# An adaLN transformer block on one core: MLP slices in groups of two, four, four, two, two, GpSimd's products of Mish regrouped, the last dense slot beside a maximum

## The chip, the core and the metric

The kernel runs on one core of a Trainium2 chip. The metric is the device time of one execution in microseconds (us); less is better. A core has the engines TensorE (PE, with its weight loads PEld), VectorE (DVE), ScalarE (ACT), GpSimd (POOL) and SyncE (SP), each with its own queue of instructions that it takes in order; SP's queue here holds the loads and stores. The matrix products go into PSUM, of which there are eight banks of 128 x 512 fp32.

## The reference

One block with adaptive layer norm: attention over 2048 positions with 32 heads of 16, then an MLP with Mish. Three of the six rows of `mod` shift, scale and gate each half.

```python
mod = (silu(c) @ w_mod)                      # sa, ca, ga, sb, cb, gb
h = layernorm(x) * (1 + ca) + sa             # x: 2048 x 512
q, k, v = (h @ wqkv) split in 32 heads of 16
o = softmax(q @ k.T * 16**-0.5) @ v
x = x + ga * (o @ wo)
h = layernorm(x) * (1 + cb) + sb
u = h @ w1 + b1                              # w1: 512 x 1792
x = x + gb * ((u * tanh(softplus(u))) @ w2)  # w2: 1792 x 512
```

## The kernel before

**Precision.** Dense products are made from a high and a low part of each operand, three matmuls for one. The splitting is a copy (`hi_copy`, L95) and a subtract (`lo_sub`, L98), mostly on GpSimd.

**The main loop.** After a first stage that makes q, k and v there are 32 iterations `n` (4 query blocks of 512 rows by 8 groups of 4 heads) of 16 steps each, T = 512 steps. A step `t` issues four score products (`score`, L507, each followed on ACT by an exp into `pr`, L513), four products for the row maxima of the iteration 20 steps ahead (`max_tile`, L470, each followed on DVE by a reduce, L472), and the products of the probabilities of step t − 2 with the values (`pv`, L531, 8 matmul instructions). `neg_max` (L481) joins the maxima of an iteration, a transposition (L487) turns them. Scores and maxima take turns in a ring of six PSUM banks; the banks "ms" and "acc" hold the dense unit at work and the values' sums.

**Dense work beside it.** A score or maximum uses 64 of PE's 128 rows. On the other 64 runs a half-height dense matmul (`mm_half`, L132), six "slots" in most steps, written between the scores and maxima. The order within the step is `mine` with `beside` in `step`: maximum, dense, score, dense and so on. A dense unit (128 or 512 columns by three partial products) of 12 slots fills four steps, a smaller one two. The first dense matmul of the next half is made to wait for `cur["after"]`, the instruction that reads the product in the last slot's place.

**The MLP as units.** The MLP of query blocks 0 to 2 runs in the main loop of the following query block: four `wo` units with their transpositions (`tr_unit`, L840), then 14 `up` units, one for each slice `f` of 128 columns of w1, and `down` units, one for each group of slices and each of four row blocks. An end of a unit calls `fin`: a bias on ACT for an up (L726), a copy on ACT (L882) and an add on GpSimd (L883) for a down. The MLP of the last query block, and the last downs of block 2 (`held`), run in the tail, whole-height (`mm`, L126).

**Mish.** With e = exp(min(u, 10)), Mish is u times e(e+2) / (e(e+2)+2). The stages of an up that ends at half step h stand in hooks, `at(h + i, stage)`, two half steps to a step: clamp (GpSimd, L732) at +1, power (ACT, L738) +3, product (GpSimd, L746 to L748) +4, log (ACT, L751) +9, inverse (ACT, L754) +13, quotient (GpSimd, L763 to L767) +13, then the places and the split of the result (L95, L98) +16 and +18. Within a half step the hooks run in the order in which they were entered. The order of each engine's instructions is that of the program text; no scheduler moves them.

**Around it.** `evac` copies an iteration's output `ot`, spreads its row sums over DMA (`rb`) and multiplies, copies and subtracts in `norm` (L574, L95, L98) on GpSimd. Weights come split from DRAM by `load_wo`, `load_w1`, `load_w2`, entered at the ends of certain units.

Of the kernel before, what the change touches and what calls it, by code (L numbers as in the profile page):

```python
# [18 lines left out]
def adaln_block(ctx: ExitStack, tc: tile.TileContext, x, wqkv, wo, w1, b1, w2, c, w_mod, out):  # L19
# [442 lines left out]
    def max_tile(n, j, s, qs, kb):  # L462

        if n not in mxs:
            mxs[n] = ap.tile([P, 2, 8, 4], F32, tag="mx", name="mx", bufs=2)

        def product():
            kt, qt = ka[(2 * n + j) % NR], qa[(2 * n + j) % NR]
            pm = ring()
            nc.tensor.matmul(pm, qt[64 * s:64 * s + 64, qs * P:(qs + 1) * P], kt[64 * s:64 * s + 64, kb * TB:(kb + 1) * TB],  # L470
                             start=True, stop=True)
            nc.vector.tensor_reduce(out=mxs[n][:, s, 4 * j + qs, kb:kb + 1], in_=pm, op=ALU.max, axis=AX.X)  # L472

        return product

    def neg_max(n):

        mx = mxs.pop(n)
        mm = ap.tile([P, 4, 2, 4], F32, tag="mm", name="mm", bufs=2)
        for v in range(2):  # L480
            nc.vector.tensor_reduce(out=mm[:, :, v, :], in_=mx.rearrange("p s (j q) k -> p (s j) q k", j=2), op=ALU.max,  # L481
                                    axis=AX.X)
        ats.setdefault(16 * n + 16 - PRO, []).append(lambda: max_rows(n, mm))
# [19 lines left out]
    def score(n, j, s, kc):  # L503
        def product():
            kt, qt = ka[(2 * n + j) % NR], qa[(2 * n + j) % NR]
            p_ = ring()
            nc.tensor.matmul(p_, kt[64 * s:64 * s + 64, kc * P:(kc + 1) * P], qt[64 * s:64 * s + 64, :],  # L507
                             start=True, stop=True)
# [4 lines left out]
            e = nc.scalar.activation(pr, p_, AF.Exp, scale=SCALE)  # L513
            if (h, b) in exps:
                tc.declare_no_dep(e.ins, exps[h, b].ins, reason="the values' product between them reads it")
            exps[h, b] = e
            pts[16 * n + kc, 2 * j + s] = pr
            return e
        return product
# [19 lines left out]
    def evac(n):  # L539
# [30 lines left out]
        if g % 2 == 1 or n == NIT - 2:  # L570
            r = slice(0, P if g % 2 else 64)

            def norm():
                nc.gpsimd.tensor_mul(od[r], od[r], rb[r])  # L574
                oh, ol = o_hl[qb]
                hi_copy("p", oh[r, g // 2, :], od[r])
                lo_sub("p", ol[r, g // 2, :], od[r], oh[r, g // 2, :])
            at(2 * t1 + (29 if g == 1 else 17 if hurry else 23), norm)
# [133 lines left out]
    def mish(f, acc, tail):  # L712
# [15 lines left out]
        def clamp():  # L728
            if tail:
                nc.scalar.activation(buf("ee", 2), b["hb"], AF.Relu, bias=hcap, scale=-1.0)  # L730
            else:
                nc.gpsimd.tensor_scalar(buf("ee", 2), b["hb"], HCAP, 0.0, op0=ALU.min, op1=ALU.add)  # L732
# [7 lines left out]
        def product():  # L740
            hb, ee, rr = b["hb"], b["ee"], buf("rr", 2)
            if tail:
                nc.vector.scalar_tensor_tensor(ee, ee, 2.0, ee, op0=ALU.add, op1=ALU.mult)
                nc.vector.tensor_mul(hb, hb, ee)
            else:
                nc.gpsimd.tensor_scalar(rr, ee, 1.0, 2.0, op0=ALU.mult, op1=ALU.add)  # L746
                nc.gpsimd.tensor_mul(ee, ee, rr)  # L747
                nc.gpsimd.tensor_mul(hb, hb, ee)  # L748
# [7 lines left out]
        def quotient():  # L756
# [5 lines left out]
            else:  # L762
                nc.gpsimd.tensor_scalar(ee, ee, 1.0, 2.0, op0=ALU.mult, op1=ALU.add)  # L763
                nc.gpsimd.tensor_mul(ee, ee, rr)  # L764
                nc.gpsimd.tensor_scalar(ee, ee, -1.0, 2.0, op0=ALU.mult, op1=ALU.add)
                nc.gpsimd.tensor_mul(rr, rr, ee)
# [17 lines left out]
    GROUPS = [list(range(a, min(a + 4, FT))) for a in range(0, FT, 4)]  # L784
    blocks = []

    def block(qb, t0):
# [39 lines left out]
        def tr_unit(i):  # L827
# [7 lines left out]
            def fin(h):  # L835

                def scaled():
                    hf = mst["p"].tile([P, TB], F32, tag="ee", name="hf2", bufs=2).rearrange("p (k m) -> p k m", m=P)
                    for k in range(DK):
                        nc.scalar.activation(hf[:, k], acc[:, k * P:(k + 1) * P], AF.Identity,  # L840
                                             scale=modc[:, 3, k:k + 1], bias=modc[:, 2, k:k + 1])
                    s = slice(i * P, (i + 1) * P)
                    hi_copy("p", hx[0][:, :, s], hf)
                    lo_sub("p", hx[1][:, :, s], hf, hx[0][:, :, s])

                at(h, scaled)
# [4 lines left out]
        def up_unit(f, tag):  # L851
# [16 lines left out]
        def down_unit(gi, i, tag=None, acc=None):  # L868
# [8 lines left out]
            if gi == 2 and i == 3 and not held and then:  # L877
                load(cur["h"] + 5, then["wo"], load_wo, range(2))

            def fin(h):  # L880
# [3 lines left out]
                if gi == len(GROUPS) - 1:  # L884
# [5 lines left out]
                    put() if held else at(h + 4, put)  # L890
                if held:
                    return
                if gi < 2 and i == 3:
                    load(h + 1, w2s, load_w2, range(6 + 4 * gi, 10 + 4 * gi))
                if then and gi == 2 and i == 0:
                    load(h + 1, then["y"], lambda j: load_y(qb + 1, j), range(3))
                if then and gi == 2 and i == 3:
                    load(h + 1, then["wo"], load_wo, range(2, DK))
                if then and gi == 3 and i == 0:
                    load(h + 10, then["y"], lambda j: load_y(qb + 1, j), range(3, 4))  # L900
                if then and gi == 3 and i == 3:
# [15 lines left out]
        if qb == NB - 2:  # L917
            mst["held"] = lambda j, acc: down_unit(2 + j // 4, j % 4, None, acc)
# [3 lines left out]
    def all_blocks():  # L922
# [3 lines left out]
        for qb, b in enumerate(blocks):  # L926
            wo, up, down = (b["units"][k] for k in ("wo", "up", "down"))
            before = blocks[qb - 1]["units"]["down"] if qb else lambda gi, i: None
            before(3, 0)
            for i in range(4):  # L930
                wo(i)
            for i in range(1, 4):
                before(3, i)
# [29 lines left out]
    def tail():  # L963
# [42 lines left out]
        for js in ((0, 1), (2,)):  # L1006
# [3 lines left out]
        fins = held((3,))  # L1010
# [102 lines left out]
    def step(t):  # L1113
# [27 lines left out]
        if t >= T:  # L1141
# [6 lines left out]
            return  # L1148
        if tm < T:
# [3 lines left out]
            mine = [x for p in zip(mo, own) for x in p] + own[len(mo):]  # L1153
        else:
# [9 lines left out]
        def emit(product):  # L1164
            e = product()
            if e is not None and cur.pop("want", None):
                cur["after"] = e

        for i in range(max(len(mine), len(beside))):
            if i == len(mine) // 2:  # L1170
                run_hooks(2 * t + 1)
            if i < f:
                last = i + 1 == f
                if i < len(mine) and mine[i] and not last:
                    emit(mine[i])
                for m in beside[i]:
                    mm_half(m, second, cur["first"], bool(second and last and m is beside[i][-1] and not cur["left"]),
                            cur.pop("after", None))
                    cur["first"] = False
                if last:  # L1180
                    cur["want"] = True
                    if i < len(mine):
                        emit(mine[i])
# [149 lines left out]
```

## Time and profile before

| what | value |
|---|---|
| runs | 1756.39, 1763.5, 1764.14 us, median 1763.5 |
| profiled execution, its own time | 1760.91 us |
| its span, first to last instruction | 1759.1 us |
| mean granted TensorE clock | 0.988 |
| DMA, mean over the span | 136 GB/s |
| DVE's reduces of maxima, L472 | 2048 of 682 ns |
| ACT's exps of scores, L513 | 2048 of 606 ns |

The page gives for each engine its busy time and its share of the span. The chain of waits follows the last instruction back to what released it, and gives the share of the span that each engine has on it. A row of a group reads "line engine operation out<-in, shape, xcount | busy us, mean ns of one | idle us of the engine just before them and what ended it". A row of the waits reads "who <- for whom: us in all, times, the longest". A row of the timeline reads "start us, us, engine, line, operation, xcount, [idle before <- releaser]". A row of the windows reads "from:to length", then for each engine its busy time and (xcount), at last the granted clock, the DMA share and GB/s; with a line given, it counts that line's instructions alone.

### The profile page before, as it was taken

What the parts mean: (1) busy time and instruction counts of PE and PEld (TensorE: products, weight loads), DVE (VectorE), ACT (ScalarE), POOL (GpSimd) and SP (SyncE); (2) the same over time, 40 slices, a digit from 0 to 9 for tenths busy, and PEclk for the clock granted to TensorE, in tenths of its full rate; (3) what the DMA queues carried; (4) which work ended last, traced back from release to release, by engine and by line L of the source; (5) the groups of instructions that cost most, each with busy time, mean ns of one, the idle gap of its engine ahead of it and who ended that gap; (6) DMA issues with size and microseconds to landing.
All of it is one profiled execution on the core that took longest, in us unless ns stands there. A gap on an engine that the chain in (4) does not pass through costs nothing.

```text
span 1759.1 us, 32844 instructions
## 1 busy us (share of the span) xinstructions
PE 1703.3 (97%) x12236; PEld 973.7 (55%) x12236; DVE 1423.9 (81%) x2384; ACT 1345.7 (77%) x2593; POOL 921.1 (52%) x898
## 2 busy tenths in 40 slices
PE   6999999999999989999999989999999989999999
PEld 5755655555345555555545555555545555554677
DVE  6988888888888878888878878888878878882367
ACT  6257777777779878888879878888878878888464
POOL 5245234666213497656524597656423696666452
PEclk9999999999999999999999999999999999999999
DMA  7777458777844332434532633524442533423252
GB/s 248 190 232 207 117 162 240 220 224 222 254 105 113 98 90 65 119 98 100 132 106 67 185 101 74 129 82 119 120 99 79 166 91 90 133 63 136 95 215 73
DMA packets 113992, 240.03 MB, mean 136 GB/s; under 512 B 24048, under 2 KB 49648, under 8 KB 107784
## 3 DMA queue, kind: packets, MB, share of 16 engines
q1 hardware_dynamic: 113832, 237.92, 47.6%
q8 instruction: 97, 1.59, 0.4%
q14 instruction: 63, 0.52, 0.1%
HBM read 179.95 MB, written 51.44 MB: 132 GB/s over the span
## 4 chain that ended last, share of the span: by engine, by line
PE 77%; DMA 10%; POOL 4%; ACT 3%; DVE 3%; SPq 2%; issue 1%; POOLq 0%; ACTq 0%; DVEq 0%
PE bk L531 25%; PE ring L470 18%; PE ring L507 17%; PE bk L132 11%; PE ring L126 2%; DMA qscr<-ql 2%; ACT pr L513 2%; PE ring L1047 1%; DVE mx L472 1%; DMA w2scr<-hl 1%; DMA kscr<-ql 1%; PE bk L126 1%; DMA vg<-vscr 1%; DMA hl<-in_B_w 1%; DMA ka<-kscr 1%
## 5 line engine op out<-in xcount | busy, mean ns | idle before, releaser
L472 DVE TENSOR_REDUCE mx<-ring 128x1 f32<-128x512 f32 x2048 | 1273.2, 682 | 225.7 <-PE ring L470 180.6
L513 ACT ACTIVATE pr<-ring 128x512 f32<-128x512 f32 x2048 | 1100.9, 606 | 263.4 <-PE bk L132 148.1
L470 PE MATMUL ring<-ka,qa 64*128 64x512 f32 x2048 | 843.1, 425 | 0.7 <-ACT hf L840 0.4
L507 PE MATMUL ring<-qa,ka 64*128 64x512 f32 x2048 | 725.9, 401 | 7.2 <-ACT pr L513 6.7
L470 PEld LDWEIGHTS ring<-ka,qa 64*128 64x128 f32 x2048 | 369.3, 185 | 408.0 <-DVE mx L472 349.3
L531 PE MATMUL bk<-pr,vg 128*32 128x512 f32 x4096 | 551.8, 611 | 0.0
L507 PEld LDWEIGHTS ring<-qa,ka 64*128 64x128 f32 x2048 | 374.2, 186 | 84.1 <-ACT pr L513 45.8
L132 PE MATMUL bk<-h,w 64*128 64x512 f32 x1008 | 283.0, 413 | 15.2 <-ACT pr L513 15.2
L132 PE MATMUL bk<-w,a_h 64*128 64x512 f32 x576 | 193.8, 416 | 0.8 <-ACT pr L513 0.5
L132 PEld LDWEIGHTS bk<-h,w 64*128 64x128 f32 x1008 | 176.1, 187 | 25.8 <-ACT pr L513 20.8
L531 PEld LDWEIGHTS bk<-pr,vg 128*32 128x32 f32 x4096 | 81.5, 108 | 140.4 <-issue 132.9
L132 PE MATMUL bk<-w,a_l 64*128 64x512 f32 x288 | 113.2, 393 | 0.0
L764 POOL TENSOR_TENSOR ee<-ee,rr 128x512 f32<-128x512 f32 x42 | 53.8, 1280 | 108.5 <-ACT rr L754 107.2
L883 POOL TENSOR_TENSOR y<-yd,y 128x512 f32<-128x512 f32 x40 | 51.8, 1295 | 110.6 <-ACT yd L882 99.4
L732 POOL TENSOR_SCALAR ee<-hb 128x512 f32<-128x512 f32 x42 | 80.7, 1921 | 48.2 <-ACT hb L726 45.2
L132 PEld LDWEIGHTS bk<-w,a_h 64*128 64x128 f32 x576 | 95.5, 184 | 7.1 <-ACT pr L513 3.3
L132 PE MATMUL bk<-w,o_hl 64*128 64x512 f32 x288 | 85.1, 426 | 7.4 <-POOL o_hl L95 6.5
L98 POOL TENSOR_TENSOR a_l<-hb,a_h 128x512 fp32r<-128x512 f32 x53 | 71.7, 1354 | 4.4
L132 PEld LDWEIGHTS bk<-w,o_hl 64*128 64x128 f32 x288 | 51.6, 193 | 12.6 <-POOL o_hl L95 7.8
L574 POOL TENSOR_TENSOR od<-od,rb 128x512 f32<-128x512 f32 (+1 forms) x16 | 20.6, 1289 | 71.3 <-DMA vg<-vscr 57.9
L132 PE MATMUL bk<-h_h,wl 64*128 64x512 f32 x168 | 56.9, 419 | 0.0
L747 POOL TENSOR_TENSOR ee<-ee,rr 128x512 f32<-128x512 f32 x42 | 54.1, 1289 | 3.5
(205 smaller groups left out, 1841.8 us busy)
## 6 DMA issues: line engine op xcount, KB each, us to landing
ka<-kscr SPq DMA_DIRECT2D x124, 384.0 KB
w<-w2scr SPq DMA_DIRECT2D x56, 512.0 KB
w<-w1scr SPq DMA_DIRECT2D x46, 512.0 KB
vg<-vscr SPq DMA_DIRECT2D x32, 552.0 KB
qa<-qscr SPq DMA_DIRECT2D x124, 100.0 KB
kscr<-qh SPq DMA_DIRECT2D x16, 512.0 KB
qscr<-qh SPq DMA_DIRECT2D x32, 256.0 KB
hl<-in_B_w SPq DMA_DIRECT2D x28, 256.0 KB
```

Source lines behind the costliest of these rows:

```text
L98: (nc.gpsimd if eng == "p" else nc.vector).tensor_sub(lo, src, hi.bitcast(F32))
L126: nc.tensor.matmul(acc, l, r, start=start, stop=stop)
L132: i = nc.tensor.matmul(acc, l[64 * g:64 * g + 64], r[64 * g:64 * g + 64], start=start, stop=stop)
L470: nc.tensor.matmul(pm, qt[64 * s:64 * s + 64, qs * P:(qs + 1) * P], kt[64 * s:64 * s + 64, kb * TB:(kb + 1) * TB], start=True, stop=True)
L472: nc.vector.tensor_reduce(out=mxs[n][:, s, 4 * j + qs, kb:kb + 1], in_=pm, op=ALU.max, axis=AX.X)
L507: nc.tensor.matmul(p_, kt[64 * s:64 * s + 64, kc * P:(kc + 1) * P], qt[64 * s:64 * s + 64, :], start=True, stop=True)
L513: e = nc.scalar.activation(pr, p_, AF.Exp, scale=SCALE)
L531: nc.tensor.matmul(accs[n][32 * h:32 * h + 32, :], vgs[n][:, o:o + 32], pts.pop((t, h)), start=(kc == 0), stop=(kc == 15))
L732: nc.gpsimd.tensor_scalar(buf("ee", 2), b["hb"], HCAP, 0.0, op0=ALU.min, op1=ALU.add)
L747: nc.gpsimd.tensor_mul(ee, ee, rr)
L764: nc.gpsimd.tensor_mul(ee, ee, rr)
L883: nc.gpsimd.tensor_add(y[i], yd, y[i])
```

## The change

The text changes in seven places.

1. `GROUPS`: the 14 slices go into groups 0–1, 2–5, 6–9, 10–11, 12–13 instead of 0–3, 4–7, 8–11, 12–13. There are five downs for each row block instead of four; a down of two slices takes two steps, one of four slices four. `all_blocks` queues five ups first, then downs and ups in a new pattern. The tail takes ten held downs instead of eight. Loads of w2, wo and y are entered at other units' ends.
2. Mish on GpSimd: `clamp` is a single min instead of min and add 0; `product` no longer multiplies u by e(e+2); `quotient` is made of a multiply, one tensor_scalar 2 − 2r, a subtract and the two products with u.
3. From up 5 on, power and product stand at +5 and +6 instead of +3 and +4.
4. `step`: where the last dense slot stood beside a score, the score moves one slot ahead and a maximum stands there. `cur["after"]` is then the reduce of that maximum.
5. At the end of a dense unit, the exp of the score in the slot before is held back until `fin` has written the bias or the copy.
6. `neg_max` joins the maxima with one reduce instead of two; `norm`'s three operations go into three hooks; `tr_unit` scales at once.
7. The store of an output row block goes to a hook that `clear` moves past an iteration's end.

**PE.** The first step with dense work beside it (h_h and h_l are the normed input; wh and wl the parts of a weight), before:

```order
L132 MATMUL bk<-h_h,wl 128x512
L470 MATMUL ring<-ka_633,qa_108 128x512
L132 MATMUL bk<-h_l,wh 128x512
L507 MATMUL ring<-qa_106,ka_104 128x512
L132 MATMUL bk<-h_l,wh 128x512
L470 MATMUL ring<-ka_633,qa_108 128x512
L132 MATMUL bk<-h_l,wh 128x512 x2
L507 MATMUL ring<-qa_107,ka_105 128x512
L531 MATMUL bk<-pr_0_1175,vg 32x512
```

and now:

```order
L132 MATMUL bk<-h_h,wl 128x512
L470 MATMUL ring<-ka_633,qa_108 128x512
L132 MATMUL bk<-h_l,wh 128x512
L506 MATMUL ring<-qa_106,ka_104 128x512
L132 MATMUL bk<-h_l,wh 128x512
L506 MATMUL ring<-qa_107,ka_105 128x512
L132 MATMUL bk<-h_l,wh 128x512 x2
L470 MATMUL ring<-ka_633,qa_108 128x512
L534 MATMUL bk<-pr_0_1174,vg 32x512
```

The last score and the last maximum of the dense part have changed places; the count is the same.

**ACT.** Around the end of an up in block 0 (`pr` are the exps of scores), before:

```order
L513 ACTIVATE pr_0_1175<-ring 128x512
L513 ACTIVATE pr_0_1182<-ring 128x512
L513 ACTIVATE pr_1_1176<-ring 128x512
L726 ACTIVATE hb<-bk,b1c 128x512
L513 ACTIVATE pr_1_1183<-ring 128x512
L513 ACTIVATE pr_2_1151<-ring 128x512
L751 ACTIVATE rr<-ee,two 128x512
```

and now, for the first cycle with a down of two slices between two ups, from the bias of up 5 over the inverse of up 4 to the power of up 5:

```order
L514 ACTIVATE pr_2_1183<-ring 128x512
L728 ACTIVATE hb<-bk,b1c 128x512
L514 ACTIVATE pr_0_1174<-ring 128x512
L514 ACTIVATE pr_0_1181<-ring 128x512
L514 ACTIVATE pr_0_1148<-ring 128x512
L755 ACTIVATE rr<-rr 128x512
...
L878 COPY yd<-bk 128x512
L514 ACTIVATE pr_2_1176<-ring 128x512
L514 ACTIVATE pr_2_1183<-ring 128x512
L514 ACTIVATE pr_2_1150<-ring 128x512
L740 ACTIVATE ee<-ee 128x512
```

The bias stands ahead of the last two exps of its step instead of the last one. Eight exps and a copy stand between the inverse and the power.

**GpSimd.** The same cycle before, with quotient, clamp, split and product:

```order
L766 TENSOR_TENSOR rr<-rr,ee 128x512
L767 TENSOR_TENSOR hb<-hb,rr 128x512
L732 TENSOR_SCALAR ee<-hb 128x512
L95 TENSOR_SCALAR a_h<-hb 128x512
L98 TENSOR_TENSOR a_l<-hb,a_h 128x512
L746 TENSOR_SCALAR rr<-ee 128x512
L747 TENSOR_TENSOR ee<-ee,rr 128x512
L748 TENSOR_TENSOR hb<-hb,ee 128x512
L763 TENSOR_SCALAR ee<-ee 128x512
```

and now:

```order
L764 TENSOR_TENSOR ee<-ee,rr 128x512
L765 TENSOR_SCALAR rr<-rr 128x512
L766 TENSOR_TENSOR rr<-rr,ee 128x512
L767 TENSOR_TENSOR hb<-hb,ee 128x512
L768 TENSOR_TENSOR hb<-hb,rr 128x512
L734 TENSOR_SCALAR ee<-hb 128x512
L879 TENSOR_TENSOR y_5257<-yd,y_5257 128x512
L95 TENSOR_SCALAR a_h<-hb 128x512
L98 TENSOR_TENSOR a_l<-hb,a_h 128x512
L748 TENSOR_SCALAR rr<-ee 128x512
L749 TENSOR_TENSOR ee<-ee,rr 128x512
```

The product is one multiply shorter; the quotient ends with the two products, and the clamp of the next up stands right behind it.

The diff, its core:

```diff
@@ max_tile, neg_max @@
-            nc.vector.tensor_reduce(out=mxs[n][:, s, 4 * j + qs, kb:kb + 1], in_=pm, op=ALU.max, axis=AX.X)
+            return nc.vector.tensor_reduce(out=mxs[n][:, s, 4 * j + qs, kb:kb + 1], in_=pm, op=ALU.max, axis=AX.X)
-        for v in range(2):
-            nc.vector.tensor_reduce(out=mm[:, :, v, :], ...)
+        twice = bass.AP(tensor=mx.tensor, offset=mx.offset, ap=[list(mx.ap)[0], [16, 4], [0, 2], [4, 4], [1, 4]])
+        nc.vector.tensor_reduce(out=mm, in_=twice, op=ALU.max, axis=AX.X)
@@ score @@
-        def product():
+        def product(hold=False):
...
-            e = nc.scalar.activation(pr, p_, AF.Exp, scale=SCALE)
+            def power():
+                e = nc.scalar.activation(pr, p_, AF.Exp, scale=SCALE)
...
+            return power if hold else power()
@@ norm (in evac) @@
+            k, d = 2 * t1 + (29 if g == 1 else 17 if hurry else 23), 0 if hurry else 2
+            at(k, lambda: nc.gpsimd.tensor_mul(od[r], od[r], rb[r]))
+            at(k + d, lambda: hi_copy("p", oh[r, g // 2, :], od[r]))
+            at(k + 2 * d, lambda: lo_sub("p", ol[r, g // 2, :], od[r], oh[r, g // 2, :]))
@@ mish @@
-                nc.gpsimd.tensor_scalar(buf("ee", 2), b["hb"], HCAP, 0.0, op0=ALU.min, op1=ALU.add)
+                nc.gpsimd.tensor_scalar_min(buf("ee", 2), b["hb"], HCAP)
...
                 nc.gpsimd.tensor_scalar(rr, ee, 1.0, 2.0, op0=ALU.mult, op1=ALU.add)
                 nc.gpsimd.tensor_mul(ee, ee, rr)
-                nc.gpsimd.tensor_mul(hb, hb, ee)
...
-                nc.gpsimd.tensor_scalar(ee, ee, 1.0, 2.0, op0=ALU.mult, op1=ALU.add)
                 nc.gpsimd.tensor_mul(ee, ee, rr)
-                nc.gpsimd.tensor_scalar(ee, ee, -1.0, 2.0, op0=ALU.mult, op1=ALU.add)
-                nc.gpsimd.tensor_mul(rr, rr, ee)
+                nc.gpsimd.tensor_scalar(rr, rr, -2.0, 2.0, op0=ALU.mult, op1=ALU.add)
+                nc.gpsimd.tensor_sub(rr, rr, ee)
+                nc.gpsimd.tensor_mul(hb, hb, ee)
                 nc.gpsimd.tensor_mul(hb, hb, rr)
@@ up_unit, down_unit @@
-    GROUPS = [list(range(a, min(a + 4, FT))) for a in range(0, FT, 4)]
+    GROUPS = [list(range(a, b)) for a, b in ((0, 2), (2, 6), (6, 10), (10, 12), (12, FT))]
-                for i, s in zip((1, 3, 4, 9, 13, 13, 16, 18), stages):
+                for i, s in zip((1, 3, 4, 9, 13, 13, 16, 18) if f < 5 else (1, 5, 6, 9, 13, 13, 16, 18), stages):
-                    put() if held else at(h + 4, put)
+                    put() if held else at(clear(h + 8), put)
+                more = {(0, 3): (6, 8), (1, 3): (8, 12), (2, 3): (12, 14)}.get((gi, i))
+                if more and held:
+                    w2s.update((k, load_w2(k)) for k in range(*more))
+                elif more:
+                    load(h + 1, w2s, load_w2, range(*more))
@@ all_blocks @@
-            for f in range(6):
+            for f in range(5):
                 up(f)
-            for j in range(8):
-                down(j // 4, j % 4)
-                up(6 + j)
-            for i in range(4 if qb < NB - 2 else 0):
-                down(2, i)
+            for i in range(4):
+                down(0, i)
+                up(5 + i)
+            down(1, 0)
+            up(9)
+            down(1, 1)
+            up(10)
+            down(1, 2)
+            down(1, 3)
+            up(11)
+            down(2, 0)
+            up(12)
+            down(2, 1)
+            up(13)
+            if qb < NB - 2:
+                down(2, 2)
+                down(2, 3)
+                for i in range(4):
+                    down(3, i)
@@ tail @@
-        for js in ((0, 1), (2,)):
+        for js in ((0, 1), (2, 3)):
...
-        fins = held((3,))
+        fins = held((4, 5))
...
-        fins += held((4, 5))
+        fins += held((6, 7))
...
-        for f in held((6, 7)):
+        for f in held((8, 9)):
@@ step @@
+            kinds = [k for p in zip("m" * len(mo), "s" * len(mo)) for k in p] + ["s"] * (len(own) - len(mo))
+            swap = 2 <= f <= len(mine) and kinds[f - 1] == "s" and kinds[f - 2] == "m"
+            if swap:
+                mine[f - 2:f] = mine[f - 1], mine[f - 2]
...
+        ends = second and f and not cur["left"]
...
+                    if swap and ends and i + 2 == f:
+                        held = mine[i](True)
+                    else:
+                        emit(mine[i])
...
-                    cur["want"] = True
-                    if i < len(mine):
-                        emit(mine[i])
-                    if second and not cur["left"]:
+                    if ends:
                         cur["fin"](2 * t + 2)
                         cur["fin"] = None
+                    if held:
+                        held()
+                    cur["want"] = True
+                    if i < len(mine) and mine[i]:
+                        emit(mine[i])
```

More of the change, by code (lines that the diff above doesn't have):

```diff
@@ L512, in product @@
             pr = prs[h][b]
[L513 to L518, printed above, removed]
+            def power():
+                e = nc.scalar.activation(pr, p_, AF.Exp, scale=SCALE)
+                if (h, b) in exps:
+                    tc.declare_no_dep(e.ins, exps[h, b].ins, reason="the values' product between them reads it")
+                exps[h, b] = e
+                pts[16 * n + kc, 2 * j + s] = pr
+                return e
+            return power if hold else power()
         return product
@@ L1148, in step @@
             return
+        swap, held = False, None
         if tm < T:
@@ L1174, in step @@
                 if i < len(mine) and mine[i] and not last:
-                    emit(mine[i])
+                    if swap and ends and i + 2 == f:
+                        held = mine[i](True)
+                    else:
+                        emit(mine[i])
                 for m in beside[i]:
-                    mm_half(m, second, cur["first"], bool(second and last and m is beside[i][-1] and not cur["left"]),
+                    mm_half(m, second, cur["first"], bool(ends and last and m is beside[i][-1]),
                             cur.pop("after", None))
```

52 lines of the change are left out of this document (19 added, 33 removed).

## The prediction, made before the change was run

> **What bounds the kernel now.** I read the busy times and the chain of waits first, for the engine that sets the end.
>
> ```profile
> PE 1703.3 (97%) x12236; PEld 973.7 (55%) x12236; DVE 1423.9 (81%) x2384; ACT 1345.7 (77%) x2593; POOL 921.1 (52%) x898
> PE 77%; DMA 10%; POOL 4%; ACT 3%; DVE 3%; SPq 2%; issue 1%; POOLq 0%; ACTq 0%; DVEq 0%
> ```
>
> PE carries 77% of the chain, so an edit on another engine counts only where PE comes to wait for it. Next the table of windows for L531, the values' product. A main-loop step ends with 8 of these matmuls, so the count divided by 8, less the one cut by the window's edge, is the number of steps.
>
> ```profile
> 409.69:449.66 39.97, 14.91 (x120) 2.20 (x112) 1.00 0.73 209
> 618.03:642.46 24.43, 8.52 (x72) 1.26 (x64) 1.00 0.36 92
> 642.46:655.31 12.85, 3.00 (x24) 0.36 (x16) 0.73 0.34 77
> 655.31:898.22 242.91, 89.49 (x679) 13.22 (x672) 1.00 0.42 108
> 1007.78:1044.76 36.98, 11.53 (x88) 1.61 (x80) 0.91 0.35 87
> 1403.30:1434.18 30.88, 9.28 (x71) 1.30 (x64) 0.89 0.41 104
> ```
>
> The first window is dense work without the Mish stages: 14 steps, 2.855 us each. The fourth is a calm stretch of an MLP block: 84 steps, 2.892 us each. The second and third are the early ups of block 0: 10 steps in 37.28 us, two of which took 12.85 us at a granted clock of 0.73. The last two are the same place in blocks 1 and 2 (10 and 8 steps). Measured against 2.892 us a step they lose 8.36, 8.06 and 7.74 us: **24.2 us in three places**. The waits and the timeline name the cause.
>
> ```profile
> ACT ee L738 <- POOL ee L732: 16.0, 6, 4.4
> PE bk L132 <- ACT pr L513: 15.7, 10, 4.0
> 643.86 1.92 POOL L732 TENSOR_SCALAR ee<-hb 128x512 f32<-128x512 f32 x1
> 645.81 0.63 ACT L738 ACTIVATE ee<-ee 128x512 f32<-128x512 f32 x1 [4.44 <-POOL ee L732]
> 647.47 0.79 PE L132 MATMUL bk<-h,w 64*128 64x512 f32 x1 [3.99 <-ACT pr L513]
> ```
>
> The power (L738) stands in ACT's queue for the clamp (L732). All exps of the scores are queued behind it, and PE waits for an exp. The clamp is late because GpSimd is: one up's work took from one L746 to the next L746, 12.80 us, where an up unit is four steps, 11.57 us.
>
> ```profile
> 606.08 0.62 POOL L746 TENSOR_SCALAR rr<-ee 128x512 f32<-128x512 f32 x1 [2.82 <-ACT ee L738]
> 618.88 0.63 POOL L746 TENSOR_SCALAR rr<-ee 128x512 f32<-128x512 f32 x1
> L732 POOL TENSOR_SCALAR ee<-hb 128x512 f32<-128x512 f32 x42 | 80.7, 1921 | 48.2 <-ACT hb L726 45.2
> L765 POOL TENSOR_SCALAR ee<-ee 128x512 f32<-128x512 f32 x42 | 26.1, 621 | 3.7
> L766 POOL TENSOR_TENSOR rr<-rr,ee 128x512 f32<-128x512 f32 x42 | 54.1, 1287 | 3.5
> L698 POOL TENSOR_SCALAR xn<-y,ln_s 128x512 f32<-128x512 f32 x10 | 7.7, 772 | 1.1
> ```
>
> **GpSimd's work and the clamp.** Per up the change drops one tensor_scalar (0.62 us) and keeps five tensor_tensors. The clamp loses its "add 0". The trace has no single min, so its price is bounded by the dearest and the cheapest one-input row: 1.92 (min and add, L732) and 0.62 (multiply and add, L765). I take 0.77, the dearest one-input row that is not itself a min (L698), because min is the only operation of GpSimd here that costs more, and one of its two passes goes. The up's work is then 12.80 − 0.62 − 1.15 = 11.0 us, and 12.2 us if the clamp stays at 1.92. At 11.0 GpSimd keeps up with four steps; at 12.2 it does not.
>
> [...]
>
> **The norm and the early ups.** The norm of the attention's output is a multiply, a copy and a subtract on GpSimd, 1.30 us for the first and with the rows above 0.62 and 1.29 for the others, 3.4 us with the gaps, and it falls into these ups.
>
> ```profile
> 631.68 1.30 POOL L574 TENSOR_TENSOR od<-od,rb 128x512 f32<-128x512 f32 x1
> ```
>
>  With 0.5 us to spare in each of three cycles, 1.8 us of it is still late at up 4's clamp; at 0.62 it is 1.3, at 1.92 it is 5.3. What PE feels of a late ACT is less, because banks of the ring are free for a while:
>
> ```profile
> 702.36 0.49 PE L132 MATMUL bk<-w,a_h 64*128 64x512 f32 x1
> 702.55 0.38 PE L507 MATMUL ring<-qa,ka 64*128 64x512 f32 x1
> 702.74 2.48 DVE L472 TENSOR_REDUCE mx<-ring 128x1 f32<-128x512 f32 x4 [0.41 <-PE ring L470]
> 702.97 2.19 ACT L513 ACTIVATE pr<-ring 128x512 f32<-128x512 f32 x4 [0.18 <-PE ring L507]
> 703.00 0.39 PE L507 MATMUL ring<-qa,ka 64*128 64x512 f32 x1
> 703.84 0.39 PE L470 MATMUL ring<-ka,qa 64*128 64x512 f32 x1
> 705.15 0.50 PE L132 MATMUL bk<-w,a_h 64*128 64x512 f32 x1
> 705.49 0.39 PE L507 MATMUL ring<-qa,ka 64*128 64x512 f32 x1
> ```
>
> The ring has six banks. The bank of the score at 702.55 is free when its exp ends at 703.57, and the sixth ring product after it starts at 703.84: 0.27 us of room. The score at 703.00 has its exp done at about 704.1 and its bank is used again at 705.49: 1.4 us. One bank of a step has the small room and three have over 1 us, so I let **1.0 us** of lateness pass unseen (bounds 0.27 and all of it). Up 4 then stalls 0.8 us, three times: 2.4.
>
> **The new wait.** The first group has two slices, so from up 5 to up 8 a two-step down stands between ups. In these six-step cycles the inverse of up f−1 and the clamp of up f come in the same half step, and GpSimd takes the quotient first. The quotient now carries five operations and ends with both products.
>
> ```profile
> 697.74 0.62 ACT L754 ACTIVATE rr<-rr 128x512 f32<-128x512 f32 x1
> 698.51 1.28 POOL L764 TENSOR_TENSOR ee<-ee,rr 128x512 f32<-128x512 f32 x1 [5.09 <-ACT rr L754]
> ```
>
> From the inverse's start: 0.77 us to the quotient's start, 6.1 us for it (four tensor_tensors of 1.29, one tensor_scalar of 0.62, gaps of about 0.08), 0.15 us of handing over, then the clamp. ACT reaches the power eight exps after the inverse, two steps or 5.7 us. The power is late by 0.77 + 6.1 + 0.15 − 5.7 = 1.3 us plus the clamp, 2.1 us at 0.77. Behind it on ACT stand the next exps, and PE and the values' products wait for these. Less the 1.0 us of room this is 1.1 us a turn, four turns a block, three blocks: **+13 us** (none if the room covers it; 25 if there is no room). From up 9 on the cycle has eight steps, the clamp comes first, and no wait arises.
>
> **The dense slot and the copies.** The count of matmuls is the same. The first dense matmul of the next half no longer waits for the exp of the score in the last slot but for the reduce of a maximum. In the rows above the third of the four reduces, 0.62 us each, ends at 704.60 and the next dense starts at 705.15, so this wait is covered by 0.55 us; moving that maximum back one slot (0.23 us) leaves it covered, as DVE takes the reduces one behind another anyway. What is gained is seen where a bias stands ahead of the last exp:
>
> ```profile
> 701.62 0.68 ACT L726 ACTIVATE hb<-bk,b1c 128x512 f32<-128x512 f32 x1
> 702.19 0.60 ACT L513 ACTIVATE pr<-ring 128x512 f32<-128x512 f32 x1
> ```
>
> The dense matmul at 702.36 started behind that exp. The most this edit can give back is the difference of the calm stretch to the stretch without Mish, 2.892 − 2.855 = 0.037 us for each of some 390 dense steps, 14.4 us. The least is nothing, as the same rows put the max's reduce ahead. Part of the difference is the transposition and ACT's added work, which stay. I take half, **−7**. The bias now stands ahead of two exps instead of one, so a copy that is late holds back one exp more; the 1.0 us of room covers its 0.69.
>
> **Downs, loads and tail.** There are 20 downs a block instead of 16, so four more ACT copies and GpSimd adds, eight of each in the loop.
>
> ```profile
> L882 ACT COPY yd<-bk 128x512 f32<-128x512 f32 x39 | 22.8, 585 | 0.0
> L481 DVE TENSOR_REDUCE mm<-mx 128x16 f32<-128x64 f32 x64 | 11.1, 214 | 1.1
> ```
>
> PE's slots are the same, and the copies lie beside them. If PE felt a tenth of each, it would be +0.5, which I take (none to 4.7, all of them). The joined maximum takes 32 of the small reduces from DVE, at most 6.8 us where DVE is 81% busy and off the chain: nothing. The norm's three operations only come apart. Loads of w2, wo and y shift in SP's queue. At a block's start wo, qa and ka still stand ahead of rb there, so the wait seen next stays as it is (nothing gained):
>
> ```profile
> 900.54 1.26 POOL L574 TENSOR_TENSOR od<-od,rb 128x512 f32<-128x512 f32 x1 [6.11 <-DMA vg<-vscr]
> 1676.18 0.59 ACT L882 COPY yd<-ring 128x512 f32<-128x512 f32 x1 [1.40 <-POOL y L883]
> 1678.17 0.59 ACT L882 COPY yd<-ring 128x512 f32<-128x512 f32 x1 [1.40 <-POOL y L883]
> 1678.81 3.05 PE L126 MATMUL ring<-h,ka 128*128 128x512 f32 x12 [0.34 <-ACT yd L882]
> ```
>
> In the tail the held downs are ten instead of eight. Their copies go one at a time, every 2.0 us, behind GpSimd's add, and the bank of the last but one frees the up at 1678.81. In the new order four such copies instead of three come before the transposes and six instead of five behind them, so the up stands one or two turns later, 2.0 to 4.0 us. I take **+2.9**, the middle, as GpSimd's add hides part of the second.
>
> **The sum.** The profiled execution took 1760.9 us (span 1759.1). −24.2 + 2.4 + 13 − 7 + 0.5 + 2.9 = −12.4, so 1748.5, **1748 us**. The three runs shown have their median at 1763.5, 2.6 us above the profiled one; I leave the forecast on the profiled scale, 0.8% under the median.
>
> **Rivals.** *The new wait is hidden.* If the ring gives 2 us, as three of four banks nearly do, the 13 and the 2.4 vanish: 1760.9 − 24.2 − 7 + 3.4 = **1733**. For it: a wait of ACT meets PE only through a bank or the values' products, two steps later, now that the dense matmul no longer waits for an exp. Against it: the one bank with 0.27 us.
>
> *The clamp stays at 1.92 us (the other side).* The min itself may be the slow part, and the row shows nothing else. Then the power waits 3.2 us in each of the twelve six-step cycles, 2.2 after the room, 26.4 us; up 4 loses 4.3 three times, 13 us; −24.2 + 26.4 + 13 − 7 + 3.4 = +11.6, 1772.5, and with half of the room 1780: **1776**. Stalls of that length also had the clock at 0.73 in the window above. It ends above the time before once the clamp takes more than some 1.4 us.
>
> *No room, and no gain from the slots.* At 629.70 the trace of before has a power 0.93 us late, and the step there took 1.0 us longer, so the lateness may come through whole: 12 × 2.1 + 3 × 1.8 = 30.6 instead of 15.4, hence **1764** with the swap's 7 and 1771 without it. The second row here is that step, in the windows for L531.
>
> ```profile
> 629.70 0.63 ACT L738 ACTIVATE ee<-ee 128x512 f32<-128x512 f32 x1 [0.93 <-POOL ee L732]
> 629.77:633.64 3.87, 1.06 (x16) 0.16 (x8) 1.00 0.84 176
> ```
>
> Against it: there the dense matmul still waited for an exp.
>
> **How the numbers follow.** Chances: the forecast 0.40, the hidden wait 0.20, the slow clamp 0.22, no room 0.18. One can tell 0.5% from no change here, so faster means below 1754.7 and slower above 1772.3. The forecast's own range is 1738 to 1761 (the swap 0 to 14, the tail, half of the room either way); three quarters of it is faster (0.30), the rest the same (0.10). The hidden wait is all faster (0.20). The slow clamp is 0.17 slower and 0.05 the same; no room is 0.13 the same and 0.05 slower. Faster 0.50, same 0.28, slower 0.22. The range takes in the hidden wait and most of the slow clamp: 1728 to 1778.
>
> **What would show it.** The clamp's group row gives its price: near 0.77 the forecast stands, near 1.92 the rival. The pair of power and clamp in the waits should count about 12 short ones (some 2 us) for ups 5 to 8 instead of 6 of up to 4.4. The steps of 9.1 us should be gone and the calm steps be at 2.87 or less. PE's waits for an exp ahead of a dense matmul should vanish; if those for a reduce appear in their place, the swap moved the wait only. The forecast is wrong if the clamp costs over 1.4 us, if the room is nothing or all, or if a DMA of the regrouped loads comes late, which no row of before shows.

## The result, and the profile after

The changed kernel took 1782.84 us (median of four runs, 1780.51 to 1785.04) where the kernel before took 1762.79 on the same chip: ratio 1.0121, 95% interval 1.0091 to 1.0151. It is slower by 20 us. The span of the profiled execution grew from 1759.1 to 1778.7 us, by 19.6.

The page's busy times and its chain of waits, in the form shown of the kernel before:

```profile
PE 1701.5 (96%) x12236; PEld 935.5 (53%) x12236; DVE 1428.9 (80%) x2352; ACT 1344.0 (76%) x2605; POOL 887.3 (50%) x868
PE 72%; POOL 10%; DMA 8%; ACT 4%; DVE 2%; issue 2%; SPq 2%; POOLq 0%; ACTq 0%; DVEq 0%
```

GpSimd is busy 34 us less, and yet its share of the chain went from 4% to 10%. Less work on an engine did not mean that fewer others wait for it. Next the same views that named the cause before: the waits, the group of the clamp, and the windows for the values' product over five steps of block 0, a sixth in block 1, and the calm stretch behind them (60 steps).

```profile
ACT ee L740 <- POOL ee L734: 38.6, 15, 2.7
L734 POOL TENSOR_SCALAR ee<-hb 128x512 f32<-128x512 f32 x42 | 62.4, 1485 | 66.7 <-ACT hb L728 64.0
640.30:646.08 5.78, 1.07 (x16) 0.16 (x8) 1.00 0.40 101
663.10:669.25 6.15, 1.47 (x16) 0.20 (x8) 0.80 0.00 0
684.11:690.65 6.54, 1.45 (x15) 0.20 (x8) 0.74 0.32 61
704.84:711.27 6.43, 1.32 (x16) 0.20 (x8) 0.73 0.72 169
725.46:732.05 6.59, 1.07 (x15) 0.16 (x8) 0.74 0.01 4
1100.99:1106.12 5.13, 1.06 (x15) 0.16 (x8) 1.00 0.99 216
732.05:903.34 171.29, 63.92 (x487) 9.43 (x480) 1.00 0.44 114
```

The power waits 15 times instead of 6, five times a block: at up 4 (the first of the five steps of block 0) and at ups 5 to 8 (the four behind it). Those are the places of the forecast, but each costs far more than forecast. The calm stretch has 171.29/60 = 2.855 us a step; the same 60 steps took 173.34 before (2.889):

```profile
724.88:898.22 173.34, 63.92 (x487) 9.44 (x480) 1.00 0.47 121
```

One of the turns in the timeline, with the inverse of up 5, GpSimd's quotient and clamp, the power of up 6, and PE:

```profile
677.38 0.62 ACT L755 ACTIVATE rr<-rr 128x512 f32<-128x512 f32 x1
678.14 1.28 POOL L764 TENSOR_TENSOR ee<-ee,rr 128x512 f32<-128x512 f32 x1 [8.31 <-ACT rr L755]
...
682.82 1.29 POOL L768 TENSOR_TENSOR hb<-hb,rr 128x512 f32<-128x512 f32 x1
684.19 1.48 POOL L734 TENSOR_SCALAR ee<-hb 128x512 f32<-128x512 f32 x1
685.71 0.63 ACT L740 ACTIVATE ee<-ee 128x512 f32<-128x512 f32 x1 [2.55 <-POOL ee L734]
686.87 0.52 PE L506 MATMUL ring<-qa,ka 64*128 64x512 f32 x1 [1.74 <-ACT pr L514]
687.95 0.62 PE L506 MATMUL ring<-qa,ka 64*128 64x512 f32 x1
```

The dots stand for the middle of the quotient. The chain is the one that the prediction drew: inverse, quotient, clamp, power, exps behind it, and PE waiting for a bank of the ring. GpSimd had stood idle for 8.31 us ahead of the quotient: it is not short of time here, it gets its work too late and in one piece. ACT waits 2.55 us, PE 1.74. Then PE's matmuls take 0.62 us instead of 0.39: the granted clock was half for 3.4 us (0.50 from 687.22 to 690.62). So the step is 6.54 us long, 3.70 more than a calm one.

Over the three blocks, by the lengths of these steps less those of calm ones (2.84 us, 3.06 where a transposition falls into the step), with what is left of the half clock in the step behind, the twelve turns of ups 5 to 8 cost 42.3 us; up 4's three stalls cost 10.2. The three long stalls of before are gone, −24.2. The loop as a whole is 15.4 us longer, which leaves −12.9 for all the rest of it; the dense slots and copies are the part of this that was forecast. The tail, from the last step of the loop to the end, is 4.2 us longer.

### The profile page after: what moved, and what is told of

Read it like the earlier page. It is cut to its first block, busy times and chain, and to the rows that moved or that the text cites. A ratio compares the mean times of both kernels' runs of the same rounds, so it can differ in the third digit from the quotient of the medians.

```text
span 1778.7 us, 32821 instructions
## 1 busy us (share of the span) xinstructions
PE 1701.5 (96%) x12236; PEld 935.5 (53%) x12236; DVE 1428.9 (80%) x2352; ACT 1344.0 (76%) x2605; POOL 887.3 (50%) x868
## 4 chain that ended last, share of the span: by engine, by line
PE 72%; POOL 10%; DMA 8%; ACT 4%; DVE 2%; issue 2%; SPq 2%; POOLq 0%; ACTq 0%; DVEq 0%
PE bk L534 23%; PE ring L470 18%; PE ring L506 17%; PE bk L132 8%; DMA qscr<-ql 2%; ACT pr L514 2%; PE ring L126 2%; DMA rb<-rscr 2%; POOL ee L734 2%; PE ring L1060 1%; POOL hb L768 1%; PE bk L126 1%; POOL rr L766 1%; POOL ee L764 1%; POOL hb L767 1%
## 5 line engine op out<-in xcount | busy, mean ns | idle before, releaser
L470 PE MATMUL ring<-ka,qa 64*128 64x512 f32 x2048 | 791.5, 432 | 6.5 <-ACT pr L514 5.9
L132 PE MATMUL bk<-h,w 64*128 64x512 f32 x1008 | 290.6, 419 | 8.6 <-ACT yd L878 7.1
L764 POOL TENSOR_TENSOR ee<-ee,rr 128x512 f32<-128x512 f32 x42 | 53.8, 1281 | 189.8 <-ACT rr L755 189.8
L734 POOL TENSOR_SCALAR ee<-hb 128x512 f32<-128x512 f32 x42 | 62.4, 1485 | 66.7 <-ACT hb L728 64.0
L879 POOL TENSOR_TENSOR y<-yd,y 128x512 f32<-128x512 f32 x50 | 64.2, 1283 | 52.8 <-ACT yd L878 51.2
L132 PEld LDWEIGHTS bk<-w,a_l 64*128 64x128 f32 x288 | 53.7, 187 | 4.0
L766 POOL TENSOR_TENSOR rr<-rr,ee 128x512 f32<-128x512 f32 x42 | 54.1, 1287 | 3.5
```

Source lines behind the costliest of these rows:

```text
L132: i = nc.tensor.matmul(acc, l[64 * g:64 * g + 64], r[64 * g:64 * g + 64], start=start, stop=stop)
L734: nc.gpsimd.tensor_scalar_min(buf("ee", 2), b["hb"], HCAP)
L766: nc.gpsimd.tensor_sub(rr, rr, ee)
L879: nc.gpsimd.tensor_add(y[i], yd, y[i])
```

## The experiments

Each ran beside the kernel before, whose median there was 1760 to 1763 us. Ratios are to those runs.

**e1: the clamp ahead of the quotient.** Edit of the changed kernel:

```diff
-                for i, s in zip((1, 3, 4, 9, 13, 13, 16, 18) if f < 5 else (1, 5, 6, 9, 13, 13, 16, 18), stages):
+                q = 14 if 4 <= f < 8 else 13
+                for i, s in zip((1, 3, 4, 9, 13, q, 16, 18) if f < 5 else (1, 5, 6, 9, 13, q, 16, 18), stages):
```

> The changed kernel, with the quotient of ups 4 to 7 one half step later (+14 instead of +13), so that GpSimd takes the clamp of the next up first. Theory (the loss is the power that waits behind quotient and clamp, 12 turns of 3.7 us: some 2 us of waiting and some 1.7 us of halved clock): ACT's waits of the power for the clamp fall from 15 to 3, the steps of 6.1 to 6.6 us go, about 1783 - 44 = 1739 us. Rival 1 (the loss lies in the twenty downs a block and their copies and adds, or in the tail): the waits go, but the time stays above 1770. Rival 2 (the wait only moves, to the log behind a later product): waits of the log for the product appear, 1755 to 1765.

It took 1746.32 us, ratio 0.9916 (0.9891 to 0.9940). The power's and the log's waits in this kernel, and the windows for the values' product over the step that took 6.54 us:

```profile
ACT ee L740 <- POOL ee L734: 8.1, 3, 2.7
ACT rr L752 <- POOL ee L749: 5.1, 12, 0.5
```

```profile
679.57:682.40 2.83, 1.07 (x16) 0.16 (x8) 1.00 0.69 130
```

Twelve of the fifteen waits are gone, and 36.5 us with them. One number in a table of hooks decides between 1.2% slower and 0.8% faster. What GpSimd does is the same work; only its order changed. So the turns are the loss, and rival 1 falls: the downs, copies and adds are still all there. Rival 2 is there in small: twelve waits of the log for the product, none over 0.5 us. The gain is some 6 us short of the 42.3 that the turns cost. Up 4's third stall took 6.9 us here instead of 5.8; where the rest went stays open.

**e2: a clamp of 0.62 us.**

```diff
-                nc.gpsimd.tensor_scalar_min(buf("ee", 2), b["hb"], HCAP)
+                nc.gpsimd.tensor_scalar(buf("ee", 2), b["hb"], 0.1, 0.0, op0=ALU.mult, op1=ALU.add)
```

> The changed kernel with the min of the clamp replaced by a multiplication by 0.1 (a multiply and add of 0.62 us; the Mish that comes out is another). It takes 0.87 us out of each clamp. Theory: the power waits 1.7 us instead of 2.6, PE 1.0 to 1.2 instead of 2. If a pause of that length leaves the clock at full speed, 12 turns lose 1.1 instead of 3.7 us, and up 4's stalls nearly go: about 1745. If the clock is halved all the same, 12 turns lose 2.8: about 1768. Rival (the clamp's price does not matter, the loss is elsewhere): above 1778.

It took 1749.45 us, 0.9928 (0.9903 to 0.9952). The power's waits, and the windows for two of the steps of ups 5 to 8 (the second has a transposition in it):

```profile
ACT ee L740 <- POOL ee L734: 22.6, 15, 1.7
```

```profile
680.92:685.20 4.28, 1.06 (x15) 0.16 (x8) 1.00 0.40 86
717.86:722.34 4.48, 1.07 (x16) 0.16 (x8) 1.00 0.02 5
```

The fifteen waits are all there, up to 1.7 us long, and a turn costs 4.28 − 2.84 = 1.44 us. The granted clock is 1.00 in both, where the step of 684.11 in the changed kernel has 0.74. Taking 0.87 us from the clamp took 2.1 us from the turn; by the author's estimate the difference of 1.2 us is the halved clock. It also shows that the room of the ring is small: of the 1.70 us of the turn shown first, 1.44 come through.

**e4: the old product and quotient** in the changed kernel (three and five operations as before, the min alone kept).

> The changed kernel with the old product and quotient on GpSimd (the product with three operations, the quotient with five, two of them short: 5.4 instead of 6.1 us; one operation of 0.62 us more per up). Theory: in the six-step cycles the power waits 1.9 instead of 2.55 us, so 12 turns lose 0.7 us less, or 2.4 less where the clock is no longer halved; ups 1 to 4 need 0.6 us more each, so up 4 stalls some 2 us longer: 1758 to 1780, by the clock. Rival (the regrouping has nothing to do with the loss): 1783 to 1790, the waits of the six-step cycles at 2.55 as before.

It took 1762.60 us, 1.0014 (1.0000 to 1.0027). The power's waits:

```profile
ACT ee L740 <- POOL ee L734: 29.5, 18, 4.1
```

Steps of ups 5 to 8 took 3.9 us at full clock (4.1 with a transposition), up 4's 8.6 to 9.0; the mean granted clock of the execution was 0.987. The turns' waits are shorter than expected, 1.33 us instead of 1.9. Regrouping the products shortened the cycle at up 4 and lengthened the quotient that stands ahead of the clamp at ups 5 to 8. With the clamp behind it the second counted for more: the changed kernel is 20 us slower than this one.

**e3 and e8: the dense slot and the held exp alone**, on the kernel before. e3 takes `score` and `step` of the change and the returned reduce of `max_tile`; e8 is e3 without the held exp:

```diff
-                    if swap and ends and i + 2 == f:
+                    if False:
                         held = mine[i](True)
```

> The kernel before with only the order of the last dense slot and the held exp taken over from the change. Theory (these two edits give what the calm steps gained, 2.89 to 2.84 us): the calm steps fall to 2.84, GpSimd's three long stalls stay, about 12 to 17 us less, 1748 (ratio 0.992). Rival (the calm steps gain because GpSimd's queue is lighter, not by the order): 1760 to 1764, calm steps 2.89.

> The kernel before with the last dense slot beside a maximum (and the wait on its reduce), but without the held exp: bias and copy come after that exp again. Theory 1 (the gain of e3 is that the dense matmul no longer waits for an exp): as e3, 1747 to 1749. Theory 2 (it is the bias that comes earlier): near before, 1757 to 1762, first steps of a unit at 2.96 us.

e3 took 1747.59 us, 0.9920 (0.9899 to 0.9941); e8 1749.84 us, 0.9935 (0.9914 to 0.9957). The windows for the 60 calm steps, of e3 and of e8:

```profile
729.41:900.61 171.20, 63.93 (x488) 9.44 (x480) 1.00 0.47 123
```

```profile
719.54:891.59 172.05, 63.92 (x487) 9.44 (x480) 1.00 0.47 123
```

2.853 and 2.868 us a step against 2.889 before. The order gives 0.021, the held exp another 0.015. In time the two kernels cannot be told apart; in the steps of the two traces they can (0.85 us over these 60 steps, 0.9 over the same 60 of block 1). Some 12 us come from these edits, with GpSimd as slow as before.

**e11: the other way round**, the change without swap and hold (`swap = False`).

> The changed kernel with the score back in the last dense slot, and so without the held exp: all the rest stays. Theory (swap and hold are worth what they were worth alone, 12 to 14 us, and the groups lose it): about 1783 + 13 = 1796, or some 10 us more where the dense matmul waits for the late exps. Rival (with the groups the swap itself makes the 12 stalls, since the maximum takes the score's bank): 1750 to 1775.

It took 1792.81 us, 1.0177 (1.0158 to 1.0197), and its 60 calm steps took 172.77 us. Without the swap the change is 10 us slower, so the gain adds up with the rest, and the swap does not make the stalls.

**e6: the groups of before.** e3 with `clamp`, `product` and `quotient` of the change; groups, their order, the hooks +3 and +4, the norm, the joining of the maxima, `tr_unit`, the stores and the loads are those of before.

> The kernel before with the swap and the held exp (e3) and the change's clamp and products, but the groups, orders and norm of before. GpSimd's cycle then is 12.8 - 0.62 - 0.44 = 11.7 us against 11.4 of PE. Theory (the regrouped slices make the new waits and are not needed once GpSimd is faster): no waits in later cycles, one of 2 to 4 us a block at up 4 or 5 where the norm falls, 1748 - 24 + 3 x 3 = about 1733. Rival (only the regrouping takes GpSimd's backlog away): three long stalls a little shorter than before, 1741 to 1747.

It took 1735.04 us, 0.9877 (0.9830 to 0.9923); its four runs reach from 1730.91 to 1748.15. Its waits of the power for the clamp:

```profile
ACT ee L742 <- POOL ee L736: 10.1, 6, 2.9
```

One step of 5.5 to 6.6 us a block is left, at up 4. The faster clamp and products end the backlog by themselves. What the change has beyond this kernel, the regrouped slices above all, turned a gain of some 26 us into a loss of 20. By e1, 36 of these 48 us hang on the place of the quotient ahead of the clamp. This kernel's tail has the length of before, so the tail's 4.2 us come with what it leaves out, of which the ten held downs are the part that stands in the tail. The other 7 or so are not traced to one edit.

**e5: the norm out of up 4's way**, on e1: the copy and the subtract of the second group's norm stand at k + 7 and k + 8.

> The kernel with the clamp ahead of the quotient (e1), and the norm's copy and subtract of the second group (1.9 us on GpSimd) put behind up 4's clamp. Theory (up 4's power waits 2.7 us because the norm stands ahead of its clamp): the wait falls to about 0.8 us, which PE does not feel; the steps of 5.8, 7.1 and 6.9 us go, 1746 - 10 = 1736. Rival (GpSimd is behind by its products, not by the norm; or SP's next output rows, which need the same buffer, come late): steps of 4 us and more stay, 1742 to 1748.

It took 1745.05 us, 0.9911 (0.9887 to 0.9934), no better than e1. The step at up 4 fell from 5.8 to 3.9 us as expected, but a step nine steps later, with up 5's log in it, now takes 6.2. ACT and GpSimd in the timeline there:

```profile
667.36 0.72 ACT L753 ACTIVATE rr<-ee,two 128x512 f32<-128x512 f32 x1 [2.12 <-POOL ee L750]
```

```profile
665.35 0.62 POOL L749 TENSOR_SCALAR rr<-ee 128x512 f32<-128x512 f32 x1
666.06 1.27 POOL L750 TENSOR_TENSOR ee<-ee,rr 128x512 f32<-128x512 f32 x1
```

The log waits for the product: without the stall at up 4, GpSimd comes to up 5's product later than ACT to its log. The work was moved, and the backlog stayed. What e1's rival 2 named came in full one edit later.

**e7 and e9: the clamp on ScalarE**, as the tail has it, on the change (e7) and on e6 (e9); **e10**: e6 with the norm of e5.

```diff
-                nc.gpsimd.tensor_scalar_min(buf("ee", 2), b["hb"], HCAP)
+                nc.scalar.activation(buf("ee", 2), b["hb"], AF.Relu, bias=hcap, scale=-1.0)
...
-                nc.scalar.activation(b["ee"], b["ee"], AF.Exp)
+                nc.scalar.activation(b["ee"], b["ee"], AF.Exp, bias=hcap, scale=-1.0)
```

> The changed kernel with the clamp on ScalarE for all ups, as the tail has it (a Relu of 10 - u ahead of the power, 0.62 us of ACT per up; GpSimd loses 1.49). Theory (what PE waits for is the power, and the power for GpSimd): the power has nothing on GpSimd left to wait for, the 12 turns go, up 4's stalls too or nearly, about 1735. Rival (the wait moves to the Relu, whose buffer the quotient of two ups before must free, or to the log behind the product): ACT waits of 1 to 3 us at the Relu or the log, 1750 to 1775.

> e6 (groups of before, swap, held exp, the change's products) with the clamp on ScalarE as in e7. Theory (of e6 only up 4's stall is left, 5.5 to 6.6 us steps, and it is a power that waits for GpSimd's clamp): the three stalls go, about 1735 - 8 = 1727. Rival (the Relu takes its own time on ACT and waits for its buffer): stalls at up 4 stay or 56 Relus of 0.62 us show in the calm steps, 1735 or more.

> e6 with the second group's norm split as in e5: its copy and subtract behind up 4's clamp. Theory: up 4's power waits 1 us instead of 2.9, steps of 3.9 instead of 5.5 us, and since here the product stands four steps ahead of the log, no wait of the log follows: about 1729. Rival (as in e5 the 1.9 us of GpSimd come back as a wait of the log for the product): about 1735.

e7 took 1740.69 us, 0.9879 (0.9852 to 0.9906), 6 us above its expectation: with nothing on GpSimd ahead of the power, all fifteen waits go, although the groups stay. e9 took 1732.07 us, 0.9833 (0.9815 to 0.9851), e10 1732.92 us, 0.9839 (0.9819 to 0.9859). e9 has the best median of all kernels; that it is better than e6 or e10 is not shown, as the intervals overlap. Its steps at up 4 are down to 3.4 us. e10's steps there are 3.4 us, but the next up's power, four steps on, waits instead, and its step takes 4.9 to 5.5 us; the rival of its expectation was right in kind, with the power in the log's place:

```profile
653.35 0.63 ACT L742 ACTIVATE ee<-ee 128x512 f32<-128x512 f32 x1 [2.28 <-POOL ee L736]
```

## Why the prediction was wrong, point by point

**What bounds the kernel: right.** PE, and the power behind GpSimd's clamp. The 9.1-us stalls of before shrank to 5.5 to 6.6 us with the faster clamp and products (e6), and went with the clamp on ScalarE (e9).

**The price of the clamp: wrong size.** Taken at 0.77 us, bounded by 0.62 and 1.92; measured 1.485. The row chosen was the nearest among operations that are not a min, and the only row with a min was the better one to go by. A single min takes 1485 ns, a multiply and add 620. That the min and the add are two passes of which one can be saved was an estimate that no run shows: leaving the add out took 0.44 us of 1.92, where 1.15 was forecast. The prediction had named a clamp of over 1.4 us as the sign that it is wrong, and it came.

**The new wait: right place, right chain, wrong price.** Twelve turns were forecast and came. With the measured clamp, lateness by the prediction's own sum is 1.3 + 1.49 = 2.8 us; 2.55 was measured. The failing steps are the next two terms.

The first is the room of 1.0 us. Turns at full clock show what it was: 1.33 us of wait cost 3.90 − 2.84 = 1.06 us (e4), 1.70 cost 1.44 (e2), and the 2.56 us of the turn below, whose step took 5.13 us at clock 1.00, cost 2.29. Each time 0.26 or 0.27 us passed unseen. That is the 0.27 us of the tightest bank, a row that the prediction shows; the room of the other three did not help.

```profile
1102.59 0.63 ACT L740 ACTIVATE ee<-ee 128x512 f32<-128x512 f32 x1 [2.56 <-POOL ee L734]
```

The second is the halved clock, which the sum of the turns put at nothing, though the prediction itself quotes the window of 12.85 us at 0.73. Together 3.5 us a turn were paid where 1.1 was forecast, 42.3 instead of 13. Of the 29 us between, the longer wait is 12 × 0.45 = 5, the room 12 × 0.73 = 9, and some 15 are left for the clock (eleven turns of 1.2 to 1.4 us are 13 to 15). The clamp's price has a part in the last too: with the short clamp of e2 the clock was 1.00 in the two steps shown.

**Up 4: right cause, wrong path and size.** 10.2 us instead of 2.4. GpSimd's clamp is late there as forecast, but PE did not wait through the ring: the first dense matmul of the next unit waits for the copy of the finished down (the first wait named in this row of the groups), and that copy stands behind the late power. The prediction counted a late copy only for the exps behind it, and let the room cover these. Here nothing was covered: 2.71 us of wait made the step 5.78 − 2.84 = 2.94 us longer.

```profile
L132 PE MATMUL bk<-h,w 64*128 64x512 f32 x1008 | 290.6, 419 | 8.6 <-ACT yd L878 7.1 <-ACT pr L514 1.5
```

**The dense slot and the held exp: right, too small.** −7 was taken, bounds 0 and 14; alone they gave 12.5 (e3), in the change 10 (e11), and the rest of the loop's account, which has other things in it too, is −12.9.

**The tail: right direction.** +4.2 us, where 2.9 was taken between 2.0 and 4.0, so a little over the upper bound.

**The rivals.** The slow clamp gave 1776 and had the mechanism; by its own sum it reaches 1780 with half of the room and some 1787 with none, and the time lies between. That it came so near is partly luck: its clamp of 1.92 us was dearer than the measured one, and it named the halved clock without a price. The rival without room had the better row, the step that lost 1.0 us to a power 0.93 us late; it kept the clamp at 0.77 and left the clock out. The slow clamp was given a chance of 0.22. The waits of the power and the missing 9.1-us steps, named as signs, both appeared. The range ended at 1778, 5 us short; the miss would have been larger, had the dense slots not given back 3 to 5.5 us more than was taken.

## What to carry to other kernels

When an engine with time to spare is to be made faster, look at the order of its queue as well: an operation that another engine waits for at once must not stand behind one that is wanted much later. Price a wait by the tightest buffer on its way, and by what the waiting engine does afterwards too; here a wait of 2.55 us cost 3.5. Where the row for a price does not exist, let the row with the same operation lead, and test a bundle by its parts, since here one part gave 12 us, one 12 more and the rest took 48.

## What the runs showed of the hardware that was not expected

In these kernels a min on GpSimd costs far more than a multiply and add: 1485 ns for min alone, 1921 for min and add, 620 for multiply and add, over the same 128 x 512 elements. So "add 0" behind the min cost 0.44 us.

PE's granted clock was half for 3.4 us after eleven of the twelve turns of ups 5 to 8, in which PE had stood still for 1.7 to 2.0 us (the window of 684.11 shows 0.74). After one it was not (the window of 1100.99, clock 1.00), though its chain and its pause of 1.75 us are the same, and that step was 1.2 to 1.4 us shorter than the others of ups 6 and 7. In e2, where a turn cost 1.44 us and the power waited 1.7 us at most, the clock was 1.00 in the two steps shown, and 0.994 in the mean of the execution against 0.984 in this one. The length of the pause is not all: up 4's three pauses were longer, 2.39, 2.31 and 2.39 us, and the half clock followed only the second, whose step took 7.13 us instead of 5.78.

In this trace they differ in where the pause falls. All 16 stretches of half clock in this trace start on one grid of 3.413 us, to 1 ns. Here are slots of that grid, with the busy time of PE in each and its clock: two that hold the pauses at 684.11 and at block 1's up 4, each with the slot behind it, and two that hold the larger part of the pauses at 1100.99 and at block 0's up 4, with the slots behind these.

```profile
683.80:687.21 3.41, 1.67 (x12) 1.00 0.67 125
687.22:690.62 3.40, 3.40 (x16) 0.50 0.01 2
1035.38:1038.78 3.40, 1.09 (x11) 1.00 0.17 37
1038.80:1042.20 3.40, 3.40 (x17) 0.50 0.90 199
1100.23:1103.63 3.40, 1.79 (x14) 1.00 0.99 225
1103.65:1107.05 3.40, 3.29 (x24) 1.00 0.78 182
639.43:642.83 3.40, 1.88 (x13) 1.00 0.09 19
642.85:646.25 3.40, 2.55 (x21) 1.00 0.70 171
```

Over the fifteen places of this trace, the clock was half in the next slot in each of the twelve where PE had been idle for 1.68 us or more of one slot, and in none of the three where the grid had cut the pause so that no slot held more than 1.63. By these places a difference of a fraction of a microsecond in where a turn falls was worth 1.2 to 1.4 us. This is read from these fifteen places alone and is no threshold for others: the half clock at 455.1 us followed a slot with 1.52 us of idle. PE was not idle for the whole of such a slot: the two ahead of the half clock above have 1.67 and 1.09 us of work in them.
